# Transposing queries and attention outputs by DMA instead of by matrix engine in a fused attention and expert kernel

## The chip, the cores and the metric

The kernel runs on one core of a Trainium2 chip. The core has five engines with instruction streams of their own: TensorE (PE, matmuls and the weight loads that go before them), VectorE (DVE), ScalarE (ACT), GpSimd (POOL) and SyncE (SP), and 16 DMA engines that move data between HBM and the on-chip memory SBUF. Each instruction stream is worked off strictly in its order. DMAs are started by instructions on a stream: here the plain ones by SP ("SPq" in the profile, hardware queue q1), and those that convert f32 to f16 on the way by POOL (software queue q0). PE writes only to PSUM; what is in PSUM has to be copied ("evacuated") by DVE or ACT before PE or a DMA can use it.

The metric is the time of one execution on the device in microseconds. The median over repeated executions is compared.

## What is computed

The reference is a sorted block attention followed by a mixture of four experts. Cut to what matters:

```python
# q, k, v: (4, 8, 768, 64)   sort_net: (4, 8, 8, 8)
P = sinkhorn(sort_net)                       # 5 rounds of row and column normalisation
k_sorted = einsum('bhij,bhjcd->bhicd', P, k_blocks)     # 8 blocks of 96 tokens
v_sorted = einsum('bhij,bhjcd->bhicd', P, v_blocks)
scores = q_blocks @ k_sorted.T / 8           # inside a block: 96 x 96
attn = softmax(scores)
attn_out = attn @ v_sorted                   # (4, 8, 768, 64)
x = attn_out.transpose(0, 2, 1, 3).reshape(3072, 512)
p = domain_probs / domain_probs.sum(-1)      # (3072, 4)
out = sum(p[:, e] * (relu(x @ w1[e]) @ w2[e]) for e in range(4))   # w1: 512x1024, w2: 1024x512
```

Every token may stand anywhere on the chip, as long as its row of `out` is written to the right place; softmax and the sum over values don't depend on the order of the keys, if values have the same order.

## The kernel before

**Stages.** Four batches. Batch 0 is worked in halves by special functions (`h_k`, `h_v`, `h_s`, `h_a`, `h_x`, `q_half`), because nothing can cover it. Then comes the long stretch in which PE does the expert matmuls of one batch, and the attention of the next batch is cut into small pieces that are put between them. In the first such stage the experts of batch 0 run as twelve-or-so microsecond units (`expert`, lines 540 and 554) with the attention of batch 1 between them. Afterwards batch b runs in three chunks of 256 tokens (`chunk`, lines 620 to 680): eight groups of 16 matmuls of 128x256 into `ps_h` (line 629), each followed by a DVE instruction (line 635) and DVE sums (lines 610 to 616), and then seven products of 16 matmuls into `ps_p` (line 656), combined by DVE, ACT and POOL (lines 669 to 680). The attention of batch b+1 lies between these. The last batch has nothing between.

**Order.** The order of every engine's instructions is the order of the program text (`manual_schedule`); there is no scheduler. `run` hands out "slots": after each group of matmuls `slot()` is called and pops the next pieces of the list `fill`, so many that the list is used up a few slots before the end. `attention_order(b)` makes that list: 24 pieces, v, v, q, k, v, v, and then for each pair of heads `pr` scores (`st_s`), the next pair's `st_q` and `st_k`, attention times values (`st_a`) and the transposition of the result (`st_x`), which is put behind the scores of the next pair.

**The pieces.**
- `st_v` (line 283): two matmuls, evacuated into `vo`; after every second pair SP writes `vo` to a scratch tensor in HBM (`vs_dram`, line 300) and reads it back in another layout (`vs`, line 305). The read waits on SP until the write is complete.
- `st_q` (line 311): 12 PE transposes (matmuls against an identity, line 315) of the queries of a pair of heads into `ps_q`, evacuated into `qT` (line 319), by DVE for batch 1 and by ACT for batches 2 and 3 (`evac`).
- `st_k` (line 322): 12 matmuls that mix and transpose the keys, evacuated into `kT` (line 334).
- `st_s` (line 339): 16 matmuls of `kT` and `qT` (line 344), then exp on ACT (line 351).
- `st_a` (line 368): 16 matmuls (line 376), then per head a reciprocal and a multiplication on DVE, which write `xsl` (lines 360 and 361).
- `st_x` (line 384): 8 PE transposes of `xsl` (line 390) into `ps_x`, evacuated into `xT` (line 393), by the same engine as in `st_q`. `xT` of a batch is what its experts read, in every chunk.

PSUM tiles of these pieces rotate through two buffers (`psA`), those of the experts through two others (`psM`).

**Tokens.** Partition p holds the six consecutive tokens 6p to 6p+5 (`load_natural`, line 79), so rows of 1,536 bytes are read from HBM, 512 of them for a load of four heads. The evacuations undo that order where the blocks of 96 are needed; within `xT` tokens are in the order (r, i, c), and rows of `out` are written with a stride of six rows (line 667).

**Loads.** POOL issues, in this order, the loads of batch 0, w1 and w2 of experts 0 and 1, after the start the k, v and q of batch 1 (lines 723 to 725) and w1 and w2 of experts 2 and 3. Those of batch b+1 are issued by `stage` right after the pieces of batch b that used the buffers (line 502); there are two buffers each. POOL also makes the permutation matrices (`builds`, 4 instructions for a batch) and the sums of w2 blocks for the products (`weight_sums(e)`, 4 instructions each, tile `T_e`).

**Expert weights per token.** `domain_probs` is loaded at the start by SP (lines 168 and 175), normalised by `mix_weights` (5 small DVE instructions) after the first half of batch 0; `spread_weights`, put into the fill list of batch 1 after its tenth piece, transposes it, writes it to `p_dram`, and `load_p` (line 597) reads 512 KB of it for each chunk, broadcast over partitions, into `pb` (one buffer).

Of the kernel before, what the change touches and what calls it, by code (L numbers as in the profile page):

```python
# [17 lines left out]
def kernel(  # L18
# [57 lines left out]

    natural = {}

    def load_natural(b, nm, qd, p0=0, pn=P):
        src = {"q": q, "k": k, "v": v}[nm]  # L80
        if (b, nm, qd) not in natural:
            natural[(b, nm, qd)] = nat.tile([P, 4, R, D], F16, name=f"nat_{nm}_{b}_{qd}", tag=f"nat_{nm}")
        t = natural[(b, nm, qd)]
        nc.gpsimd.dma_start(  # L84
            t[ds(p0, pn)].rearrange("p h r d -> p h (r d)"),
            src[b, ds(4 * qd, 4)].rearrange("h (p r) d -> p h (r d)", r=R)[ds(p0, pn)],
        )

    def head(b, nm, h):
        return natural[(b, nm, h // 4)][:, h % 4, :, :]  # L90
# [33 lines left out]
        eye16.rearrange("p (o c) -> p o c", o=1).broadcast_to([P, NB, CP]),  # L124
    )

    KH = NFC // 2
    Hb = const.tile([P, E, NFC, 2 * P], F16, name="Hb")
    Sb = const.tile([P, 4, E, KH * P], F16, name="Sb")
    Hflat = Hb.rearrange("p e f x -> p (e f x)")  # L130
# [22 lines left out]
    load_w2(0)  # L153
    load_w1(1)
    load_w2(1)
    identf = const.tile([P, P], F32, name="identf")
    nc.gpsimd.tensor_copy(identf[:], ident[:])
    nc.gpsimd.tensor_copy(
        maskv.rearrange("p (c i) -> p c i", i=NB),
        eye16.rearrange("p (c o) -> p c o", o=1).broadcast_to([P, CP, NB]),  # L160
# [1 line left out]
    for n in range(1):  # L162
# [1 line left out]
        nc.gpsimd.memset(vo[:, :, :, ds(D, 2)], 1.0)  # L164
        vos.append(vo)

    p_sb = const.tile([P, B, R, E], F32, name="p_sb")
    nc.sync.dma_start(
        p_sb[:, 1:B].rearrange("p b r e -> p b (r e)"),
        moe_domain_probs.rearrange("(b p r) e -> p b (r e)", b=B, p=P)[:, 1:B],  # L170
    )

    for r2 in range(2):
        for hf in range(2):
            nc.sync.dma_start(
                p_sb[ds(64 * r2, 64), 0, ds(3 * hf, 3), :],
                moe_domain_probs[ds(hf * HS, HS)].rearrange("(p r s) e -> p r s e", r=3, s=2)[:, :, r2, :],
            )

# [100 lines left out]
    def evac(b):  # L280
        return nc.vector.tensor_copy if b == 1 else nc.scalar.copy
# [27 lines left out]
            vss[(b, qd)] = vs  # L309

    def st_q(b, pr):
        ps = psa([P, R, P], F16, f"ps_q_{b}_{pr}")
        for r in range(R):
            for hh in range(2):
                nc.tensor.transpose(  # L315
                    ps[ds(D * hh, D), r, :], head(b, "q", 2 * pr + hh)[:, r, :], ident[:]
                )
        qT = att.tile([P, NB, R, CP], F16, name=f"qT_{b}_{pr}", tag="qT")
        evac(b)(qT[:], ps.rearrange("p r (i c) -> p i r c", c=CP))
        qTs[(b, pr)] = qT.rearrange("p i r c -> p i (r c)")  # L320

    def st_k(b, pr):
        ps = psa([P, R, P], F32, f"ps_k_{b}_{pr}")
# [59 lines left out]

    def st_x(b, pr):
        if b not in xTs:
            xTs[b] = moe.tile([P, NKC, R, NB, CP], F16, name=f"xT_{b}", tag="xT")
        ps = psa([P, NB, BLK], F16, f"ps_x_{b}_{pr}")
        xsl = xsls[(b, pr)]
        for i in range(NB):
            nc.tensor.transpose(  # L390
                ps[:, i, :], xsl[:, i, :, :].rearrange("c h d -> c (h d)"), ident[0:BLK, 0:BLK]
            )
        evac(b)(
            xTs[b][:, pr, :, :, :].rearrange("p r i c -> p i r c"),
            ps.rearrange("p i (r c) -> p i r c", c=CP),
        )


# [86 lines left out]
    def attention_order(b):  # L485
        o = [(st_v, 0), (st_v, 1), (st_q, 0), (st_k, 0), (st_v, 2), (st_v, 3)]
        for pr in range(NPB):
            o.append((st_s, pr))
            if pr + 1 < NPB:
                o += [(st_q, pr + 1), (st_k, pr + 1)]  # L490
            o.append((st_a, pr))
            o.append((st_x, pr))

        for pr in range(NPB - 1):
            o.remove((st_x, pr))
            o.insert(o.index((st_s, pr + 1)) + 1, (st_x, pr))

        def stage(f, pr):
            f(b, pr)
            nm = {st_q: "q", st_k: "k", st_v: "v"}.get(f)  # L500
            if nm and pr % 2 and b + 1 < B:
                load_natural(b + 1, nm, pr // 2)

        return [lambda f=f, pr=pr: stage(f, pr) for f, pr in o]

    NR = (B - 1) * E * R
    p_dram = dramp.tile([B - 1, E, R * P], F32, name="p_dram")
    pn = const.tile([P, NR], F32, name="pn")  # L510
    pT = const.tile([NR, P], F32, name="pT")

    def spread_weights():
        ps = psa([NR, P], F32, "ps_p")
        nc.tensor.transpose(ps[:], pn[:], identf[:])
        nc.vector.tensor_copy(pT[:], ps[:])
        nc.sync.dma_start(p_dram.rearrange("b e (r p) -> (b e r) p", p=P), pT[:])
        pbs[(1, 0)] = load_p(1, 0)

    def mix_weights():  # L520
        den = const.tile([P, B, R, 1], F32, name="den")
        nc.vector.tensor_reduce(den[:], p_sb[:], AX.X, ALU.add)
        nc.vector.tensor_scalar(out=den[:], in0=den[:], scalar1=1e-9, scalar2=None, op0=ALU.add)
        nc.vector.reciprocal(den[:], den[:])
        nc.vector.tensor_tensor(p_sb[:], p_sb[:], den[:].broadcast_to([P, B, R, E]), ALU.mult)
        nc.vector.tensor_copy(pn.rearrange("p (b e r) -> p b r e", b=B - 1, e=E), p_sb[:, 1:B])

    oaccs = {}

    def expert(b, e, hf, slot):  # L530
# [19 lines left out]
        for t in range(n // P):  # L550
            col = (R // 2) * hf + t
            ps = psm([P, Dm], F32, f"ps_o_{b}_{e}_{col}")
            for fc in range(NFC):
# [1 line left out]
                    ps[:], hT[:, fc, ds(t * P, P)], w2sb[e][:, fc, :],  # L555
                    start=(fc == 0), stop=(fc == NFC - 1),
                )
            pcol = p_sb[:, b, col, ds(e, 1)]
            if e == 0:
                oaccs[(b, col)] = moeo.tile([P, Dm], F32, name=f"oacc_{b}_{col}", tag="oacc")  # L560
                nc.vector.tensor_scalar(
# [14 lines left out]

    DH = Dm // 2
    Ts = []  # L580

    def weight_sums(e):
        t = const.tile([P, 3, KH, DH], F16, name=f"T_{e}")
        w = w2sb[e]
        b11, b12 = w[:, 0:KH, 0:DH], w[:, 0:KH, DH:Dm]
        b21, b22 = w[:, KH:NFC, 0:DH], w[:, KH:NFC, DH:Dm]
        t2, t3, n4 = t[:, 0], t[:, 1], t[:, 2]
        tt = nc.gpsimd.tensor_tensor
        tt(t3, b22, b12, ALU.subtract)
        tt(b12, b12, b11, ALU.subtract)  # L590
        tt(t2, b22, b12, ALU.subtract)
        tt(n4, b21, t2, ALU.subtract)
        Ts.append({
            "b11": b11, "b21": b21, "b22": b22, "t1": b12, "t2": t2, "t3": t3, "n4": n4,
        })

    def load_p(b, c):
        pb = moe.tile([P, E, 2 * P], F32, name=f"pb_{b}_{c}", tag="pb", bufs=1)
        nc.sync.dma_start(
            pb[:],  # L600
            p_dram[b - 1, :, ds(2 * c * P, 2 * P)].rearrange("(o e) x -> o e x", o=1).broadcast_to([P, E, 2 * P]),
        )
        return pb

# [14 lines left out]

    def chunk(b, c, slot):  # L620

        xT = xTs[b].rearrange("p k r i c -> p k (r i c)")
        pb = pbs.pop((b, c))
        for e in range(E):
            for g in range(2):
# [38 lines left out]
        ob = moeo.tile([P, Dm], F32, name=f"ob_{b}_{c}", tag="oacc")  # L664
        p1, p5, u2, u3 = [moe.tile([P, DH], F32, name=f"{n}_{b}_{c}", tag=n, bufs=1) for n in ("p1", "p5", "u2", "u3")]
        tt = nc.vector.tensor_tensor
        o = out[ds(b * S, S), :].rearrange("(p r) d -> p r d", r=R)
        oa1, oa2, ob1, ob2 = oa[:, 0:DH], oa[:, DH:Dm], ob[:, 0:DH], ob[:, DH:Dm]
        nc.scalar.copy(p1[:], product("p1", blk(0, 0), "b11"))  # L669
        nc.scalar.copy(ob1, product("p4", blk(1, 1), "n4"))  # L670
# [42 lines left out]
    h_x(0, 0, nc.scalar.copy)  # L713
    h_a(1, 0)
    h_x(1, 0, nc.scalar.copy)
    mix_weights()
    state["start"] = False

    build_PI0(nc.gpsimd, 1, Rs[:, 0:H, HB:NB])
# [1 line left out]
        build_PI(nc.gpsimd, n, "v")  # L721
        build_PI(nc.gpsimd, n, "k")
    for qd in range(2):
        for nm in ("k", "v", "q"):
            load_natural(1, nm, qd)
    for e in range(2, E):
        load_w1(e)
        load_w2(e)
# [64 lines left out]
```

## Time and profile before

| what | value |
|---|---|
| median of 5 runs | 404.31 us (402.59 to 404.64) |
| the profiled execution, its own time | 404.2 us |
| its span on the core | 402.4 us |
| mean granted TensorE clock | 0.975 |
| instructions | 8931 |
| DMA packets, bytes | 34,059 packets, 34.38 MB |
| q0 (POOL's queue): packets, share of the 16 engines' span | 18,976, 29.2% |
| q1 (SP's queue): packets, share | 15,044, 13.3% |

The profile counts microseconds from the start of the span. The stages in it: batch 0's attention up to about 62.7, with its first expert units from 29.2 on; expert units of batch 0 with the attention of batch 1 from 62.7 to 137.2; the chunks of batch 1 with the attention of batch 2 from 137.2 to 228.0; the chunks of batch 2 with the attention of batch 3 to 318.6; the chunks of batch 3 alone to 398.5; the last outputs up to the end.

The groups that the change touches, each with its count, busy time and mean duration:

| line | engine, what | count | busy us | mean ns |
|---|---|---|---|---|
| 315 | PE transposes into `ps_q` | 144 | 6.3 | 223 |
| 390 | PE transposes into `ps_x` | 96 | 6.1 | 206 |
| 319 | ACT copies `qT` (batches 2, 3) | 8 | 6.4 | 799 |
| 319 | DVE copies `qT` (batch 1) | 4 | 2.2 | 552 |
| 393 | ACT copies `xT` (batches 2, 3) | 8 | 6.4 | 799 |
| 393 | DVE copies `xT` (batch 1) | 4 | 2.2 | 550 |
| 84 | POOL, issuing loads of q | 10 | 7.0 | 713 |

A matmul's mean duration is the time from its start to its modelled end; matmuls overlap, so 12 of them take far less than 12 times that, and what a group costs PE is read from the starts of the groups before and after it.

### The profile page before, as it was taken

How to read it: one execution, taken by the hardware profiler on the slowest of the kernel's cores; microseconds unless marked ns; L12 is line 12 of the kernel's file. 1: busy time of each engine (PE TensorE's matmuls, PEld its weight loads, DVE VectorE, ACT ScalarE, POOL GpSimd, SP SyncE). 2: the span in 40 equal slices, each digit the busy share in tenths (PEclk: the TensorE clock that was granted, in tenths of full speed). 3: DMA queues.
4: the chain of work that ended last, by engine and by line, in shares of the span. 5: the costliest groups of instructions: out<-in, count | busy, mean ns of one | idle time of the engine just before them, and what ended most of it. 6: DMA issues, size and time to landing. Idle time of an engine off the chain costs nothing.

```text
span 402.4 us, 8931 instructions
## 1 busy us (share of the span) xinstructions
PE 383.8 (95%) x3965; PEld 301.0 (75%) x3965; DVE 233.5 (58%) x418; ACT 93.8 (23%) x140; POOL 89.8 (22%) x107
## 2 busy tenths in 40 slices
PE   4779989999999999999999999999999999999996
PEld 4665555555555688888888888888888888888885
DVE  5462443452444385397388386397388395693772
ACT  2253243223432223132312123232312001000000
POOL 8452030049459430200200500100100100101001
PEclk9658999999999999999999999999999999999999
DMA  9999999993063364911151123201101101101101
GB/s 120 207 210 194 129 148 203 199 205 83 0 79 81 78 121 108 154 46 52 56 78 54 54 82 92 94 2 54 55 2 53 53 2 54 54 0 54 55 0 54
DMA packets 34059, 34.38 MB, mean 85 GB/s; under 512 B 2652, under 2 KB 28324, under 8 KB 34020
## 3 DMA queue, kind: packets, MB, share of 16 engines
q0 software_dynamic: 18976, 17.83, 29.2%
q1 hardware_dynamic: 15044, 15.97, 13.3%
q8 instruction: 31, 0.51, 0.5%
q14 instruction: 8, 0.07, 0.0%
HBM read 42.86 MB, written 8.76 MB: 128 GB/s over the span
## 4 chain that ended last, share of the span: by engine, by line
PE 82%; DVE 10%; DMA 4%; ACT 1%; issue 1%; POOL 0%; DVEq 0%; SPq 0%; ACTq 0%; POOLq 0%
PE ps_h L629 27%; PE ps_p L656 26%; PE ps_o L554 9%; PE ps_h L540 9%; DVE Hb L635 3%; DMA vs_dram<-vo 3%; DVE xsl L361 2%; DMA nat_q<-in_q_dram 2%; PE ps_k L327 1%; PE ps_q L315 1%; PE ps_s L344 1%; PE ps_w L187 1%; PE ps_x L390 1%; PE ps_a L376 1%; PE ps_v L287 1%
## 5 line engine op out<-in xcount | busy, mean ns | idle before, releaser
L629 PE MATMUL ps_h<-xT,w 128*128 128x256 f16 x1152 | 132.0, 273 | 1.0 <-DVE Hb L635 1.0
L629 PEld LDWEIGHTS <-w 128*128 128x128 f16 x1152 | 111.2, 98 | 16.0 <-issue 1.2
L635 DVE SCALAR_TENSOR_TENSOR Hb<-ps_h,pb 128x1024 f16<-128x1024 f32 x72 | 87.7, 1220 | 24.4 <-PE ps_h L629 24.3
L656 PEld LDWEIGHTS <-Sb 128*128 128x128 f16 x576 | 55.6, 98 | 7.0
L674 POOL TENSOR_TENSOR oa<-u,p 128x256 f32<-128x256 f32 x9 | 6.5, 724 | 202.9 <-issue 177.9
L540 PE MATMUL ps_h<-xT,w 128*128 128x384 f16 x256 | 47.3, 333 | 0.2 <-ACT xT L480 0.2
L656 PEld LDWEIGHTS <-Hb 128*128 128x128 f16 x432 | 41.7, 98 | 5.9 <-issue 0.6
L554 PE MATMUL ps_o<-w,Hb 128*128 128x512 f16 x192 | 44.4, 380 | 0.0
L546 ACT ACTIVATE Hb<-ps_h 128x768 f16<-128x768 f32 x32 | 26.0, 811 | 62.7 <-PE ps_h L540 62.7
L540 PEld LDWEIGHTS <-w 128*128 128x128 f16 x256 | 24.1, 99 | 16.2 <-issue 1.6
L656 PE MATMUL ps_p<-w,Sb 128*128 128x256 f16 x288 | 34.4, 273 | 0.0
L656 PE MATMUL ps_p<-w,Hb 128*128 128x256 f16 x288 | 34.4, 273 | 0.0
L656 PE MATMUL ps_p<-T,Sb 128*128 128x256 f16 x288 | 33.3, 273 | 0.0
L554 PEld LDWEIGHTS <-Hb 128*128 128x128 f16 x192 | 17.6, 98 | 19.8 <-ACT Hb L546 0.6
L565 DVE SCALAR_TENSOR_TENSOR oacc<-ps_o,p_sb,oacc 128x512 f32<-128x512 f32 x18 | 13.5, 750 | 26.8 <-PE ps_o L554 26.8
L351 ACT ACTIVATE ET<-ps_s 96x768 f16<-96x768 f32 x24 | 18.0, 802 | 36.3 <-PE ps_s L344 36.3
L361 DVE TENSOR_TENSOR xsl<-ps_a,rz 96x512 f16<-96x512 f32 x32 | 22.0, 687 | 1.1
L673 DVE TENSOR_TENSOR u<-ps_p,p 128x256 f32<-128x256 f32 x9 | 3.8, 425 | 30.4 <-PE ps_p L656 30.4
L669 ACT COPY p<-ps_p 128x256 f32<-128x256 f32 x9 | 3.4, 374 | 74.3 <-PE ps_p L656 64.3
L656 PE MATMUL ps_p<-T,Hb 128*128 128x256 f16 x144 | 17.2, 272 | 0.1
L612 DVE TENSOR_TENSOR Sb<-Sb,Hb 128x512 f16<-128x512 f16 x36 | 15.3, 425 | 1.2
L84 POOL DMA_DIRECT2D nat_v<-in_v_dram x8 | 6.1, 758 | 41.0 <-PE ps_v L287 34.5
(104 smaller groups left out, 353.9 us busy)
## 6 DMA issues: line engine op xcount, KB each, us to landing
w<-in_moe_w_dram POOLq DMA_DIRECT2D x8, 1024.0 KB, 17.7
pb<-p_dram SPq DMA_DIRECT2D x9, 512.0 KB, 4.0
nat_k<-in_k_dram POOLq DMA_DIRECT2D x8, 384.0 KB, 6.5
nat_v<-in_v_dram POOLq DMA_DIRECT2D x8, 384.0 KB, 7.4
vs_dram<-vo SPq DMA_DIRECT2D x6, 396.0 KB, 4.2
vs<-vs_dram SPq DMA_DIRECT2D x6, 396.0 KB, 4.6
nat_q<-in_q_dram POOLq DMA_DIRECT2D x6, 384.0 KB, 5.9
out_dram<-ob SPq DMA_DIRECT2D x9, 256.0 KB, 2.1
```

What stands on the lines that cost most here:

```text
L84: nc.gpsimd.dma_start(t[ds(p0, pn)].rearrange("p h r d -> p h (r d)"), src[b, ds(4 * qd, 4)].rearrange("h (p r) d -> p h (r d)", r=R)[ds(p ...
L351: nc.scalar.activation(ETs[2 * (pr % 2) + hh][:, 0:S].rearrange("c (a x) -> c a x", a=2), pss[hh][0:BLK, :, 0:HS], AF.Exp, bias=0.0, scale ...
L361: nc.vector.tensor_tensor(xsl[:, :, hh, :].rearrange("c (a i) d -> c a i d", a=2), av[:, :, :, 0:D], rz[:].broadcast_to([BLK, 2, HB, D]), ...
L540: nc.tensor.matmul(ps[:, a, 0:HS], w1sb[e][:, kc, ds((2 * f2 + a) * P, P)], xT0[hf][:, :, kc, :], start=(kc == 0), stop=(kc == NKC - 1),)
L546: nc.scalar.activation(hT[:, ds(2 * f2, 2), :], ps[:, :, 0:HS], AF.Relu, bias=0.0, scale=1.0,)
L554: nc.tensor.matmul(ps[:], hT[:, fc, ds(t * P, P)], w2sb[e][:, fc, :], start=(fc == 0), stop=(fc == NFC - 1),)
L565: nc.vector.scalar_tensor_tensor(out=oaccs[(b, col)][:], in0=ps[:], scalar=pcol, op0=ALU.mult, in1=oaccs[(b, col)][:], op1=ALU.add,)
L612: tt(sm[1], sm[0], blk(0, 0), ALU.subtract)
L629: nc.tensor.matmul(ps[:, f, :], w1sb[e][:, kc, ds((4 * g + f) * P, P)], xT[:, kc, ds(2 * c * P, 2 * P)], start=(kc == 0), stop=(kc == NKC ...
L635: nc.vector.scalar_tensor_tensor(out=Hb[:, e, ds(4 * g, 4), :], in0=ps[:], scalar=0.0, op0=ALU.max, in1=pb[:, ds(e, 1), :].broadcast_to([P ...
L656: nc.tensor.matmul(ps[:], lhs(e, f), Ts[e][rhs][:, f, :], start=(e == 0 and f == 0), stop=(e == E - 1 and f == KH - 1),)
L674: nc.gpsimd.tensor_tensor(oa2, u2[:], p5[:], ALU.add)
```

## The change

- `st_q` no longer uses PE, PSUM, DVE or ACT. SP issues one transposing DMA from the loaded queries (128 x 768 f16) into `qT` (128 x 6 x 128). `qT` has three buffers instead of two.
- `st_x` likewise: one transposing DMA from `xsl` (96 x 1024) into its quarter of `xT` (128 x 8 x 96).
- Queries of batches 1 to 3 are loaded by `load_queries`: partition p holds tokens p, 128+p, ..., so that the transposed queries come out in natural order. That takes one DMA for each head (8 a batch instead of 2) with rows of 256 bytes in HBM and 128 bytes in SBUF, into one buffer. Those of batch 1 come after k and v of batch 1 and before the weights of experts 2 and 3; those of batch b+1 are issued after the last `st_s` of batch b.
- `xT` and `out` of batches 1 to 3 are in natural token order: a store of 128 tokens writes 128 consecutive rows.
- The expert weights per token of batches 1 to 3 are loaded in natural order by one SP DMA of 2,304 rows of 16 bytes (before: 384 rows of 96 bytes) and normalised in `spread_weights`; those of batch 0 are normalised where all were before.
- To make room, the queries of batch 0 lie in tile `T_3`, and the f32 identity and the weights per token in tile `T_2`, until `weight_sums` writes these.

In the program, the two transposing DMAs stand in SP's stream where `st_q` and `st_x` stand in the order of pieces. SP's stream in the attention of batch 1 begins: write of `vs_dram`, read of `vs`, transposition of pair 0's queries, write, read, transposition of pair 1's queries, write of `p_dram`, load of `pb`, transposition of pair 0's outputs, and so on.

```diff
+    def load_queries(b):
+        t = nat.tile([P, NPB, R, 2, D], F16, name=f"natq_{b}", tag="natq", bufs=1)
+        natural[(b, "q")] = t
+        for h in range(H):
+            nc.gpsimd.dma_start(t[:, h // 2, :, h % 2, :], q[b, h].rearrange("(t p) d -> p t d", p=P))
...
     def st_q(b, pr):
-        ps = psa([P, R, P], F16, f"ps_q_{b}_{pr}")
-        for r in range(R):
-            for hh in range(2):
-                nc.tensor.transpose(
-                    ps[ds(D * hh, D), r, :], head(b, "q", 2 * pr + hh)[:, r, :], ident[:]
-                )
-        qT = att.tile([P, NB, R, CP], F16, name=f"qT_{b}_{pr}", tag="qT")
-        evac(b)(qT[:], ps.rearrange("p r (i c) -> p i r c", c=CP))
-        qTs[(b, pr)] = qT.rearrange("p i r c -> p i (r c)")
+        qT = att.tile([P, R, P], F16, name=f"qT_{b}_{pr}", tag="qT", bufs=3)
+        nc.sync.dma_start_transpose(
+            qT[:], natural[(b, "q")][:, pr].rearrange("p t h d -> p (t h d)")
+        )
+        qTs[(b, pr)] = qT.rearrange("p t x -> p (t x)").rearrange("p (i x) -> p i x", i=NB)
...
     def st_x(b, pr):
         if b not in xTs:
-            xTs[b] = moe.tile([P, NKC, R, NB, CP], F16, name=f"xT_{b}", tag="xT")
-        ps = psa([P, NB, BLK], F16, f"ps_x_{b}_{pr}")
-        xsl = xsls[(b, pr)]
-        for i in range(NB):
-            nc.tensor.transpose(
-                ps[:, i, :], xsl[:, i, :, :].rearrange("c h d -> c (h d)"), ident[0:BLK, 0:BLK]
-            )
-        evac(b)(
-            xTs[b][:, pr, :, :, :].rearrange("p r i c -> p i r c"),
-            ps.rearrange("p i (r c) -> p i r c", c=CP),
+            xTs[b] = moe.tile([P, NKC, NB, BLK], F16, name=f"xT_{b}", tag="xT")
+        nc.sync.dma_start_transpose(
+            xTs[b][:, pr], xsls[(b, pr)].rearrange("c i h d -> c (i h d)")
         )
...
+            if f == st_s and pr == NPB - 1 and b + 1 < B:
+                load_queries(b + 1)
...
+    def load_weights_of_tokens():
+        nc.sync.dma_start(pn, moe_domain_probs[S:N].rearrange("(t p) e -> p t e", p=P))
+
     def spread_weights():
+        normalized(pn, NT, "den_1")
...
-        o = out[ds(b * S, S), :].rearrange("(p r) d -> p r d", r=R)
+        o = out[ds(b * S, S), :].rearrange("(t p) d -> p t d", p=P)
...
     for qd in range(2):
-        for nm in ("k", "v", "q"):
+        for nm in ("k", "v"):
             load_natural(1, nm, qd)
+    load_queries(1)
```

## The prediction

> **What bounds the kernel now.** I read the page's engine shares and the shares of the chain of waits, then the windows by stage.
>
> ```profile
> PE 383.8 (95%) x3965; PEld 301.0 (75%) x3965; DVE 233.5 (58%) x418; ACT 93.8 (23%) x140; POOL 89.8 (22%) x107
> ...
> PE 82%; DVE 10%; DMA 4%; ACT 1%; issue 1%; POOL 0%; DVEq 0%; SPq 0%; ACTq 0%; POOLq 0%
> ```
>
> ```profile
> 62.70:137.20 74.50, 74.17 (x602) 40.50 (x601) 31.76 (x51) 24.96 (x32) 36.57 (x24) 1.00 0.62 113
> 137.20:227.95 90.75, 90.19 (x986) 77.96 (x985) 59.76 (x103) 21.87 (x33) 15.01 (x16) 1.00 0.39 80
> ```
>
> The second view gives, for a stretch, its length, then busy microseconds of PE, PEld, DVE, ACT and POOL, the granted clock, the share of the DMA engines and GB/s. In both stages that hold the pieces to be replaced PE is idle for 0.3 and 0.6 us. A piece taken from PE there shortens the time by its own length, unless PE then waits.
>
> **What the pieces cost PE.** Timeline of the second chunk of batch 1 (start, length, instructions), PE lines:
>
> ```profile
> 192.04 1.91 PE L656 MATMUL ps_p<-T,Sb 128*128 128x256 f16 x16
> 193.79 0.51 PE L390 MATMUL ps_x<-ident,xsl 96*128 96x96 f16 x8
> 194.13 1.91 PE L656 MATMUL ps_p<-T,Sb 128*128 128x256 f16 x16
> 195.88 1.91 PE L656 MATMUL ps_p<-w,Sb 128*128 128x256 f16 x16
> 197.72 0.53 PE L315 MATMUL ps_q<-ident,nat_q 128*64 128x128 f16 x12
> 198.18 1.92 PE L629 MATMUL ps_h<-xT,w 128*128 128x256 f16 x16
> ```
>
> Sixteen matmuls take 1.75 from start to start (194.13 to 195.88). With `st_x` between it is 2.09 (192.04 to 194.13), with `st_q` 2.30 (195.88 to 198.18): the pieces cost 0.34 and 0.55. There are 12 of each: 12 x 0.89 = 10.7 us off PE.
>
> Not all of it is gained. In the chain in order of time the steps from 204.2 to 218.8, and again from 294.9 to 309.5, are DVE's (lines 635 and 361), which the change doesn't relieve there. One `st_x` lies in each: 2 x 0.34 = 0.7 stays.
>
> The evacuations, 8 x 0.55 on DVE for batch 1 and 16 x 0.80 on ACT, are priced at nothing: DVE has 31.8 us of work in the 74.5 us of the first stage, ACT 21.9 in 90.8, and PE waited for neither. Fewer `psA` tiles only loosen their rotation.
>
> **What comes in their place.** A transposing DMA occurs nowhere in this trace. Its row of bounds: the shortest SP transfer lands in 2.1 us (256 KB stores), the longest in 10.7 (the first `vs_dram` write, 768 rows under load). Nearest by rows and size is that write without load, 3.4 us (issued 233.11, its reader released at 236.47); I take 3.0 for what one adds when it stands in a queue already running.
>
> Most have cover. `st_x` of the last pair is the tight one:
>
> ```profile
> 218.12 0.69 DVE L361 TENSOR_TENSOR xsl<-ps_a,rz 96x512 f16<-96x512 f32 x1
> 218.86 0.37 PEld L390 LDWEIGHTS <-xsl 96*128 96x128 f16 x8 [0.35 <-DVE xsl L361]
> 227.95 1.25 PE L629 MATMUL ps_h<-xT,w 128*128 128x256 f16 x10
> ```
>
> `xsl` is ready at 218.8 and the next chunk reads `xT` at 227.95: 9.1 us, hidden by five products; 9.1 in the next stage, 8.6 before the first chunk (128.65 to 137.23). Queries of batches 2 and 3 have 14 us from `st_q` (145.0) to `st_s` (159.0). SP issues the `vs` read at 146.0; it lands 4.8 later and the transposition by 154. So 0.
>
> The first pair of batch 1 is not covered:
>
> ```profile
> 67.21 0.40 SPq L300 DMA_DIRECT2D vs_dram<-vo  x1
> 68.66 0.53 PE L315 MATMUL ps_q<-ident,nat_q 128*64 128x128 f16 x12
> 77.90 0.33 SPq L305 DMA_DIRECT2D vs<-vs_dram  x1
> 79.51 0.21 PE L344 MATMUL ps_s<-qT,kT 64*128 64x96 f16 x1
> 79.86 0.36 SPq L300 DMA_DIRECT2D vs_dram<-vo  x1
> ```
>
> ```profile
> vs_dram<-vo SPq DMA_DIRECT2D x1, 396.0 KB, 10.7
> ...
> vs<-vs_dram SPq DMA_DIRECT2D x1, 396.0 KB, 7.7
> ...
> vs_dram<-vo SPq DMA_DIRECT2D x1, 396.0 KB, 7.0
> ```
>
> (The last view: DMA issues of the three SP lines above, KB, and us to landing.) PE made these queries at 68.7, ten microseconds ahead. In the new stream the transposition stands behind the `vs` read, which SP holds until the write has landed, so it is issued at 78.2. The read lands at 85.6. The write issued after it, at 79.86, landed at 86.9, only 1.3 behind: what follows in SP's queue comes in after what stands before. So the queries land at 85.6 + 3.0 = 88.6. PE reaches the scores at 79.5 - 0.55 + 0.4 (start, below) = 79.4 and stands for 9.2 us, and behind it in PE's order all expert matmuls. Bounds: 0.9, if the transposition passes the read and takes 2.1; 16.9, if it takes 10.7 behind it. The next pair gains from that stall: its transposition is out at about 93 and lands by 98, PE is there at 92.5 - 1.1 + 9.6 = 101: 0.
>
> A standing PE loses clock. Windows of the start, when PE became continuously busy at 30.3:
>
> ```profile
> 30.00:32.00 2.00, 1.75 (x7) 0.71 (x5) 0.00 (x0) 0.25 (x1) 0.00 (x0) 0.50 1.16 207
> 32.00:34.00 2.00, 2.00 (x40) 1.34 (x39) 0.70 (x2) 0.81 (x1) 0.08 (x1) 0.54 1.27 215
> 34.00:36.00 2.00, 2.00 (x35) 1.24 (x33) 0.62 (x1) 0.81 (x2) 0.79 (x2) 1.00 1.19 195
> ```
>
> The clock stays at 0.50 for 3.7 us of full work, which loses 1.9. I add 1.9 (bounds 0 and 1.9).
>
> [...]
>
> **Loads and the rest.** Queries: 6,144 rows a batch instead of 1,024. Between 113 and 125 us 1,056 q0 packets took 51.1% of 16 engines: 93 ns each at 1,536 bytes; between 2 and 12 us 1,235 small q1 packets took 11.5%: 15 ns each. A batch thus occupies every engine for 5.8 to 36 us (before 6.0); nearest are the 528-byte rows at 50 ns (896 packets, 25.3% of 11 us), scaled down to 30: 11.5, 5.5 more. Behind them on POOL stand w1 of expert 2, landed at 61.9 and first used at 88.4: 26 us of cover, lost by some 5 us only at the upper bound. POOL's six more issues of 0.75 are 4.5 us. Behind those of batch 2 stand `weight_sums(2)` and `builds`, whose first result (125.0 to 126.0) is used at 139.0: covered. Those of batch 3 come well before `oa` (line 674 at 225). They wait for all four transpositions of the batch before, which PE needs earlier anyway.
>
> The 2,304 rows of 16 bytes are issued at the start, when the first queries set the chain (landing at 8.5). Turn by turn with the 48 packets an engine of the first k and q loads (512 + 256 rows over 16) they add 48 x 15 ns = 0.7, and the 384 rows that go give back 0.36: +0.4 (bounds -0.3 and +1.5). Normalising later moves five DVE instructions of 1.2 us together to about 91 us; behind them `pb`, issued at 93.6 and first read at 139.2: 0. Behind the transpositions on SP stand also `pb` loads (issued 216.5, read 229.9) and stores: covered. `T_2` and `T_3` are free at about 91 and 50, written from 116 on: 0. Rows of `out` keep their 2 KB: 0.
>
> **Sum**, against the profiled run's own 404.2 (span 402.4 and 1.8 around it; 0.1 under the median): 404.2 - 10.7 + 0.7 + 0.4 = 394.6 with no stall; + 9.2 + 1.9 = **405.7**.
>
> **The rivals.**
> - *The stall is short* (faster). The queries pass the `vs` read, land like an unloaded write at 78.2 + 3.4 = 81.6, and PE stands 2.2 us without losing clock: 394.6 + 2.2 = 396.8. For it: the read's rows are few and long, and transposing traffic may not share its turns. Against: the 1.3 us between read and next write. It decides if they land before 86.5 (stall 7.1, with the clock 403.6).
> - *Transposing is slow* (slower). At 10.7 each, PE stands 16.9 + 1.9, and `xT` is late before three batches: 10.7 - 8.6 + 0.3, and twice 10.7 - 9.1 + 0.3: 6.2 in all; 419.6. It decides from about 8.6 on. For it: nothing in the trace shows its speed; against: twice the bytes take 3.4 as a copy.
> - *The removed work was not PE's to give*: DVE sets the pace throughout the chunks and 394.6 becomes 401.7 (2 x 3.56 lost), 412.8 with stall. Against: DVE works 59.8 of 90.75 us there.
>
> **How the numbers follow.** Forecast (stall between 7 and 13 us) 0.50, short stall 0.30, slow transposing 0.17, pace of DVE 0.03. The forecast's own range is 403 to 411. What this kernel's measurement can tell is about 0.3%, 1.2 us. Of the forecast's 0.50 I put 0.03 below 403.1, 0.17 within and 0.30 above 405.5; with the rivals faster 0.33, same 0.17, slower 0.50. The range goes from 396.5, which takes in most of the short stall, to 417, short of the slowest.
>
> **What would show it.** Lines 315 and 390 gone from PE and some 3.6 us less PE time in each stage; PE's `ps_s` of batch 1's first pair held by the DMA of `qT` for about 9 us near 79, with a clock of 0.50 after it; transpositions landing about 3 us after what stands before them; no wait of line 629 for `xT`. A `qT` wait under 3 us, or `xT` waits at the starts of batches, would make the prediction wrong.

## The result, and the profile after

| kernel | median | range | runs |
|---|---|---|---|
| before | 404.1 us | 402.27 to 406.13 | 50 |
| after | 406.62 us | 403.36 to 408.16 | 26 |

The ratio of after to before is 1.0054, with a 95% interval of 1.0039 to 1.0068: slower by half a per cent. Below, "before" and "after" stand for the two kernels. The profiled execution of after has a span of 404.8 us; the one of before has 402.4.

Engine shares and the shares of the chain of waits, page of after:

```profile
PE 377.1 (93%) x3725; PEld 294.9 (73%) x3725; DVE 231.8 (57%) x413; ACT 81.6 (20%) x124; POOL 105.1 (26%) x125
...
PE 84%; DVE 7%; DMA 6%; ACT 1%; issue 1%; POOL 0%; SPq 0%; DVEq 0%; ACTq 0%; POOLq 0%
```

PE works 6.7 us less than before (383.8), on 240 matmuls fewer, ACT 12.2 us less; and the span is longer. The work that went was not idle work, so PE must have waited somewhere instead. The windows by stage of after (stretch, its length, busy us of PE, PEld, DVE, ACT and POOL, granted clock, DMA share, GB/s) say in which stage:

```profile
61.77:146.60 84.83, 74.89 (x523) 39.38 (x522) 31.05 (x47) 25.07 (x32) 39.99 (x29) 0.92 0.75 119
146.60:234.05 87.45, 86.74 (x906) 75.51 (x905) 59.81 (x103) 15.67 (x25) 21.86 (x23) 1.00 0.60 101
234.05:321.15 87.10, 86.60 (x906) 75.53 (x905) 59.74 (x103) 15.67 (x25) 8.23 (x10) 1.00 0.28 74
```

The two stages of chunks are shorter by 3.30 (90.75 before) and 3.55 us (90.65). The first stage is longer by 10.33 (74.50): PE stands there for about 10 us, and the clock falls to 0.92 in the mean. With the start (0.93 us earlier in this execution) and the last stage (83.65 instead of 83.80) this adds up to the whole difference of the spans: -0.93 + 10.33 - 3.30 - 3.55 - 0.15 = 2.4.

The timeline of PE in after, where before went on at 79.5 with the scores:

```profile
75.31 2.76 PE L548 MATMUL ps_h<-xT,w 128*128 128x384 f16 x16
84.94 0.82 PE L351 MATMUL ps_s<-qT,kT 64*128 64x96 f16 x16 [6.87 <-DMA qT<-natq]
85.69 2.74 PE L548 MATMUL ps_h<-xT,w 128*128 128x384 f16 x8
88.23 4.92 PE L562 MATMUL ps_o<-w,Hb 128*128 128x512 f16 x16
...
101.42 0.40 PE L530 MATMUL ps_p<-T 128*72 128x128 f32 x1 [2.90 <-DVE T L515]
101.62 2.76 PE L548 MATMUL ps_h<-xT,w 128*128 128x384 f16 x8
```

Two waits, in brackets with what ended them. The first is the one that was looked for, 6.87 us for the transposed queries. The second, 2.90 us for the normalised weights per token, is a surprise. Behind each the same matmuls take longer than before: 16 scores 0.82, 8 of `ps_h` 2.74 and 16 of `ps_o` 4.92 us, against 0.51, 1.47 and 3.63, which is 2.9 us; behind the second wait 2.76 for 8 against 1.46 and 0.40 for one against 0.27, 1.4 us. PE in before, at the same places (its first score ran alone, at 79.51):

```profile
79.88 0.50 PE L344 MATMUL ps_s<-qT,kT 64*128 64x96 f16 x15 [0.16 <-DVE vo L294]
80.31 1.47 PE L540 MATMUL ps_h<-xT,w 128*128 128x384 f16 x8
...
82.17 3.63 PE L554 MATMUL ps_o<-w,Hb 128*128 128x512 f16 x16
...
91.12 1.46 PE L540 MATMUL ps_h<-xT,w 128*128 128x384 f16 x8
```

The windows of after show why, by the granted clock (the figure after POOL's): it fell during the wait and came back about 6 us after it.

```profile
80.00:82.00 2.00, 0.00 (x0) 0.00 (x0) 0.00 (x0) 0.00 (x0) 0.00 (x0) 0.65 1.20 298
82.00:84.00 2.00, 0.00 (x0) 0.00 (x0) 0.00 (x0) 0.00 (x0) 0.00 (x0) 0.50 1.30 130
84.00:86.00 2.00, 1.06 (x18) 0.75 (x19) 0.00 (x0) 0.21 (x1) 0.00 (x0) 0.50 0.88 204
...
90.00:92.00 2.00, 2.00 (x9) 0.86 (x8) 0.54 (x1) 0.00 (x0) 0.00 (x0) 0.79 0.34 62
```

So the first stage saves its 4 x 0.89 = 3.6 us and loses 6.87 + 2.9 + 2.90 + 1.4 = 14.1: 10.5, and 10.33 are seen.

SP's queue in after, and what its transfers of 64 to 79 us took from issue to landing (the last figure):

```profile
66.27 0.37 SPq L311 DMA_DIRECT2D vs_dram<-vo  x1
77.21 0.33 SPq L316 DMA_DIRECT2D vs<-vs_dram  x1
77.65 1.33 SPq L324 DMA_TRANSPOSE qT<-natq  x1
```

```profile
vs_dram<-vo SPq DMA_DIRECT2D x1, 396.0 KB, 10.9
vs<-vs_dram SPq DMA_DIRECT2D x1, 396.0 KB, 7.0
qT<-natq SPq DMA_TRANSPOSE x1, 7.2
```

The value write holds the read until 77.2, the transposition goes out right behind the read and lands at 77.65 + 7.2 = 84.9, only 0.7 us after the read (77.21 + 7.0 = 84.2).

The second wait, in the timelines of DVE and of POOL in after (lines 512 to 515 normalise the weights per token, lines 597 and 598 belong to `weight_sums`):

```profile
97.81 0.21 DVE L512 TENSOR_REDUCE den<-T 128x18 f32<-128x72 f32 x1
98.06 0.97 DVE L513 TENSOR_SCALAR den<-den 128x18 f32<-128x18 f32 x1
99.06 0.27 DVE L514 RECIPROCAL den<-den 128x18 f32<-128x18 f32 x1
99.36 1.91 DVE L515 TENSOR_TENSOR T<-T,den 128x72 f32<-128x72 f32 x1
```

```profile
96.87 2.12 POOL L597 TENSOR_TENSOR w<-w 128x1024 f16<-128x1024 f16 x1
99.07 2.11 POOL L598 TENSOR_TENSOR T<-w 128x1024 f16<-128x1024 f16 x1
```

DVE's line 513 ends at 99.03 and POOL's 597 at 98.99; DVE's 515 ends at 101.27 and POOL's 598 at 101.18. Two DVE instructions end with the POOL instruction that runs beside them. Lines 512 and 514 between them take 0.21 and 0.27.

### The profile page after: what moved, and what is told of

Read it like the earlier page. It is cut to its first block, busy times and chain, and to the rows that moved or that the text cites. A ratio compares the mean times of both kernels' runs of the same rounds, so it can differ in the third digit from the quotient of the medians.

```text
span 404.8 us, 8510 instructions
## 1 busy us (share of the span) xinstructions
PE 377.1 (93%) x3725; PEld 294.9 (73%) x3725; DVE 231.8 (57%) x413; ACT 81.6 (20%) x124; POOL 105.1 (26%) x125
## 3 DMA queue, kind: packets, MB, share of 16 engines
q1 hardware_dynamic: 36161, 20.70, 21.1%
## 4 chain that ended last, share of the span: by engine, by line
PE 84%; DVE 7%; DMA 6%; ACT 1%; issue 1%; POOL 0%; SPq 0%; DVEq 0%; ACTq 0%; POOLq 0%
PE ps_h L636 29%; PE ps_p L663 28%; PE ps_o L562 9%; PE ps_h L548 9%; DMA vs_dram<-vo 3%; DVE xsl L368 2%; DMA qT<-natq 2%; DVE Hb L642 2%; DMA T<-in_q_dram 1%; PE ps_k L334 1%; PE ps_s L351 1%; PE ps_w L198 1%; PE ps_a L383 1%; PE ps_v L298 1%; DVE kT L417 1%
## 5 line engine op out<-in xcount | busy, mean ns | idle before, releaser
L636 PEld LDWEIGHTS <-w 128*128 128x128 f16 x1152 | 111.9, 98 | 16.5 <-issue 2.1
L548 PE MATMUL ps_h<-xT,w 128*128 128x384 f16 x256 | 49.7, 345 | 0.2 <-ACT xT L480 0.2
L663 PEld LDWEIGHTS <-Hb 128*128 128x128 f16 x432 | 41.8, 98 | 5.9 <-issue 0.6
L548 PEld LDWEIGHTS <-w 128*128 128x128 f16 x256 | 25.0, 102 | 17.7 <-issue 3.5
L562 PEld LDWEIGHTS <-Hb 128*128 128x128 f16 x192 | 18.4, 100 | 21.8 <-issue 2.0
L103 POOL DMA_DIRECT2D natq<-in_q_dram x24 | 19.7, 860 | 0.4 <-issue 0.4
L93 POOL DMA_DIRECT2D nat_k<-in_k_dram x8 | 6.4, 794 | 45.5 <-PE ps_k L334 35.0
```

What stands on the lines that cost most here:

```text
L93: nc.gpsimd.dma_start(t[ds(p0, pn)].rearrange("p h r d -> p h (r d)"), src[b, ds(4 * qd, 4)].rearrange("h (p r) d -> p h (r d)", r=R)[ds(p ...
L103: nc.gpsimd.dma_start(t[:, h // 2, :, h % 2, :], q[b, h].rearrange("(t p) d -> p t d", p=P))
L548: nc.tensor.matmul(ps[:, a, 0:HS], w1sb[e][:, kc, ds((2 * f2 + a) * P, P)], xT0[hf][:, :, kc, :], start=(kc == 0), stop=(kc == NKC - 1),)
L562: nc.tensor.matmul(ps[:], hT[:, fc, ds(t * P, P)], w2sb[e][:, fc, :], start=(fc == 0), stop=(fc == NFC - 1),)
L636: nc.tensor.matmul(ps[:, f, :], w1sb[e][:, kc, ds((4 * g + f) * P, P)], xT[:, kc, ds(2 * c * P, 2 * P)], start=(kc == 0), stop=(kc == NKC ...
L663: nc.tensor.matmul(ps[:], lhs(e, f), Ts[e][rhs][:, f, :], start=(e == 0 and f == 0), stop=(e == E - 1 and f == KH - 1),)
```

## The experiments

The kernel before, on the same chip and at the same time, took 403.33 us for the first four runs, 403.87 for the next four and 403.83 for the last four; every ratio is against that. As the runs before differ by up to 0.2% from the 404.1 above, a difference to the changed kernel is taken from the ratios: 1.0054 less the run's own, times 404.1; each has an uncertainty of about 1 us.

### The first two transpositions ahead of the stage

```diff
     first = attention_order(1)
+    for n in (2, 7):              # st_q of pairs 0 and 1
+        first[n]()
+        first[n] = lambda: None
```

> The transpositions of pairs 0 and 1 of batch 1's queries stand ahead of all vs_dram transfers on SP, all else as in the changed kernel. Theory (the stall came from standing behind the vs write and read on SP): they land before 70 us, PE's wait of 6.9 us for qT and the half clock after it (2.9 us) go, 406.6 - 9.8 = 396.8. Rival (the load on the DMA engines by weights near 78 us, or another transfer the scores need, holds PE just as long): PE still stands near 78 us, time within 2 us of 406.6.

Measured: 399.59 us, ratio 0.9907 (0.9887 to 0.9928), 5.9 us under the changed kernel. The wait for `qT` is gone. Another, smaller one stands in the same place (PE timeline):

```profile
80.78 0.20 PE L351 MATMUL ps_s<-qT,kT 64*128 64x96 f16 x1 [1.38 <-DVE vo L305]
81.64 0.50 PE L351 MATMUL ps_s<-qT,kT 64*128 64x96 f16 x15 [0.67 <-DVE vo L305]
82.07 2.49 PE L548 MATMUL ps_h<-xT,w 128*128 128x384 f16 x8
```

The scores take over the PSUM buffers that DVE's `vo` copies empty, and these wait for the value write, which landed 12.1 us after its issue at 67.56. Before had that wait too, with 0.16 us. These waits and the slow matmuls behind them (2.49 and 4.33 us against 1.47 and 3.63) make 3.8 us, which is what is missing from the 9.8 expected. The queries were not the only thing that is late here: what delays the write is the next limit.

The second wait stays, at 2.90 us, but in this execution the matmuls behind it have their full speed (1.46 us for the 8 of `ps_h`, 0.27 for the one of `ps_p`): the same wait cost clock in after and none here.

### The normalisation early

```diff
     load_weights_of_tokens()
+    normalized(pn, NT, "den_1")
...
     def spread_weights():
-        normalized(pn, NT, "den_1")
```

> The weights per token of batches 1 to 3 are normalised directly after those of batch 0 (near 29 us) instead of in spread_weights; the query stall stays. Theory (PE's wait of 2.9 us for the normalised weights and the half clock after it cost some 4.2 us, because two of the DVE instructions wait for POOL's sums): DVE lines 513 and 515 take 0.2 to 0.3 us each, no wait of the transposition of the weights above 0.3 us, 406.6 - 4.2 = 402.4. Rival (the wait is part of the recovery from the query stall and PE only waits elsewhere): within 1 us of 406.6.

Measured: 401.3 us, ratio 0.9951 (0.9935 to 0.9967). In the new place, near 28.5 us, POOL is idle, and the two instructions take 0.18 and 0.23 us. PE goes from the matmuls before `ps_p` straight on, and the wait for `qT` stays, at 7.58 us. By the ratios this gives back 4.2 us; the trace of after had 2.90 + 1.4 = 4.3.

### Both together

> Both edits. Theory (the two waits are separate and add): 406.6 - 9.8 - 4.2 = 392.6, under the kernel before by 11.5 us; PE idle under 1 us in the stage from 62 us to the first chunk. Rival (with PE earlier the next thing is late: outputs of batch 1 not transposed in time, or POOL's permutation matrices): one of these waits appears before the first chunk, time above 395.

Measured: 396.6 us, ratio 0.9823 (0.9795 to 0.9852), 4.0 over the 392.6 expected. The two gains add up, nearly: 5.9 and 4.2 alone, 9.3 together. What is left of the stalls is PE's 1.16 and 0.66 us for `vo`, which neither expectation named, with a clock down to 0.50 from 82 to 84 us.

### The transposition ahead of the value read

```diff
     def st_v(b, pr):
...
             nc.sync.dma_start(vs_dram...)          # the write
+            if (b, pr) == (1, 1):
+                st_q(1, 0)
...
             nc.sync.dma_start(vs...)               # the read
...
     first = attention_order(1)
+    first[2] = lambda: None
```

> Only pair 0's transposition is moved, to between the vs write and the vs read on SP, so that it is issued near 67 us while the write is under way for 11 us. Theory (SP's transfers land in the order of the queue): it lands with the write or under 1.5 us after it, near 77 to 79 us, and not in the 3 to 4 us of an unloaded transposition; PE's wait at the scores is under 1 us; 396.5 to 398.5. Rival (each transfer has its own share of the engines and only their load counts): it lands well before the write, at 70 to 74 us.

Measured: 403.27 us, ratio 0.9987 (0.9961 to 1.0013), and a wait of 4.30 us. Neither expectation holds: the queries land 4.8 us after the write (66.99 + 11.3 = 78.3), not with it and not well before it. SP's line, the landing, and the packets of the two queues between 79 and 81 us:

```profile
67.46 5.08 SPq L326 DMA_TRANSPOSE qT<-natq  x1
```

```profile
qT<-natq SPq DMA_TRANSPOSE x1, 15.6
```

```profile
q0 software_dynamic: 332, 0.26, 89.2%
q1 hardware_dynamic: 332, 0.08, 42.7%
```

Issued ten microseconds sooner, the queries come only 1.8 sooner: 67.46 + 15.6 = 83.1. SP is held for 5.08 us by the issue alone.

Two things hold the transposition. One is its place behind the write: from 72 to 77 us q1 moved 691 packets beside 692 of q0, but only 102 of all these were under 512 bytes. The transposition's packets have 256 bytes and the write's 528 (by their sizes in the trace of after), so nearly all were the write's. Small packets came in number only when the write was almost through: 173 from 77 to 79 us, 348 from 79 to 81, 228 from 81 to 83. The other is the load: beside the backlog in POOL's queue q0, SP's packets of q1 went one for one with it (the 691 beside 692, and 332 beside 332 in the view above), and the change makes some 800 packets for a transposition ((36,161 - 15,044 - 1,920 more rows of weights per token) / 24). Here they take from 76 to 83 us; in after nearly all of them went between 82 and 84 us, when q1 moved 763 packets beside 75 of q0.

### PE kept at work while it waits

```diff
+    scores = first[6]
+    first[6] = lambda: (warm(112), scores())
```

> 112 matmuls that nothing reads are put on TensorE just ahead of the scores of pair 0, batch 1, so that it works through most of the 6.87 us in which it waits for qT; nothing else is changed. Theory (the wait costs twice: its own length and the half clock behind it): qT still lands at about 85 us, the scores still start within 1 us of that, but the 8 and 16 matmuls behind them (2.74 and 4.92 us in the changed kernel) take 1.5 and 3.7 us again, so about 2.9 us come back: 406.6 - 2.9 = 403.7 us. Rival (the slow matmuls have another cause, such as DMA traffic or the evacuations): they stay slow and the time stays at 406.6 us.

Measured: 403.05 us, ratio 0.9986 (0.9962 to 1.0009): 2.7 us under the changed kernel, 2.9 expected. PE timeline:

```profile
78.20 6.41 PE L198 MATMUL ps_w<-ident 128*128 128x128 f16 x112 [0.31 <-DVE vo L305]
84.97 0.51 PE L351 MATMUL ps_s<-qT,kT 64*128 64x96 f16 x16 [0.36 <-DMA qT<-natq]
85.42 1.47 PE L548 MATMUL ps_h<-xT,w 128*128 128x384 f16 x8
86.73 3.62 PE L562 MATMUL ps_o<-w,Hb 128*128 128x512 f16 x16
```

The scores start at 84.97 as they did at 84.94, so nothing came sooner; what runs behind them has the lengths of before again. The slow matmuls were the price of standing still, not of DMA traffic. The second wait is still 2.90 us here, and as in the first run the matmuls behind it are not slow (1.46 us for 8).

### The sums of weights written later

Shortened:

```diff
-        + plain(weight_sums 0, 1) + halves([(0, 2, 0), (0, 2, 1), (0, 3, 0)])
+        + halves([(0, 2, 0)]) + plain(weight_sums 0, 1) + halves([(0, 2, 1), (0, 3, 0)])
```

> The eight GpSimd instructions that make the sums of the weights of experts 0 and 1 are put behind one more half-unit of the feed-forward; the normalisation stays where the change has it. Theory (VectorE's instructions on fp32 tiles wait until GpSimd's tensor instruction ends): L513 and L515 take 0.2 to 0.3 us in their place instead of 0.97 and 1.91, TensorE's wait for the normalised weights falls from 2.90 to about 0.6 us and the half clock behind it (about 1.3 us) goes, so 406.6 - 3.6 = 403.0 us, less what the sums may cost where they now stand. Rival (the normalisation is slow where it stands whatever GpSimd does, or the place in the order alone costs the wait): L513 and L515 stay near 1 and 1.9 us and the time stays at 406.6 us.

Measured: 406.16 us, ratio 1.0061 (1.0033 to 1.0089), and this tells nothing about the cause. POOL began the sums at 94.05 us as before (94.66): it had nothing else to do, so a later place in the program did not make them later. Lines 513 and 515 took 0.96 and 1.92. A later run, below, does what this one meant to.

### The weights of expert 3 later

Shortened:

```diff
-    for e in range(2, E):
-        load_w1(e); load_w2(e)
+    load_w1(2); load_w2(2)
...
         halves([(0, 0, 1), (0, 1, 1)])
+        + plain(lambda: load_w1(3), lambda: load_w2(3))
```

> The 2 MB of weights of expert 3 are asked for about 38 us later (behind the half-unit of expert 1, at about 92 us, for a use at about 120 us); nothing else is changed. Theory (the small rows of the value write, of its read and of the transposition take turns packet by packet with GpSimd's loaded queue, and that is why they take 11, 7 and 7 us): the queue is empty some 10 us sooner, the value write issued at about 67 us lands in 4 to 7 us instead of 11, the transposition is issued at 72 to 75 us and lands 3 to 5 us later, before or within 1 us of 79.4 us, when TensorE comes to the scores; the 6.87 us and the half clock behind them go: 397 to 399 us. Rival (the transposition is late because SP hands it out behind the value write and read and because it is slow by itself): write and transposition keep their 11 and 7 us, the wait stays over 5 us and the time at 405 to 407 us. If the weights of expert 3 land too late for their use, TensorE waits there and the time says so.

Measured: 396.66 us, ratio 0.9837 (0.9814 to 0.986), 8.8 us under the changed kernel where 6.87 + 2.9 = 9.8 was to be had (397 to 399 us expected). SP's queue, the landings of its transfers issued from 72 to 77 us, the landing of the write, and PE:

```profile
66.79 0.38 SPq L311 DMA_DIRECT2D vs_dram<-vo  x1
71.71 0.33 SPq L316 DMA_DIRECT2D vs<-vs_dram  x1
72.15 1.82 SPq L324 DMA_TRANSPOSE qT<-natq  x1
```

```profile
vs<-vs_dram SPq DMA_DIRECT2D x1, 396.0 KB, 4.0
...
qT<-natq SPq DMA_TRANSPOSE x1, 4.4
```

```profile
vs_dram<-vo SPq DMA_DIRECT2D x1, 396.0 KB, 4.9
```

```profile
78.53 0.51 PE L351 MATMUL ps_s<-qT,kT 64*128 64x96 f16 x16
78.98 1.47 PE L548 MATMUL ps_h<-xT,w 128*128 128x384 f16 x8
```

Write, read and transposition take 4.9, 4.0 and 4.4 us instead of 10.9, 7.0 and 7.2, in the same order of the queue and with the same work. The queries are there at 76.6, PE comes at 78.5 and doesn't wait. So the place behind write and read is dear only with the backlog: 2 MB of weights, which after first uses at 123 us, stood in POOL's queue beside them. POOL now issues them at 85 to 87 us, and PE doesn't wait for them. Either cure ends the wait for `qT`: the transposition out of that place (the first run) or the backlog out of the way (this one). The change didn't make the backlog: in before the value write took 10.7 us at the same place. It put a transfer that PE waits for behind it.

The wait for the normalised weights stays (2.34 us), without slow matmuls behind it.

### All three

> The first two transpositions of queries ahead of the stage, the normalisation early, and the weights of expert 3 later, together. Theory: what the run with the first two left (TensorE waits 1.16 and 0.66 us for vo at 79 to 80 us, and a clock of 0.5 to 0.7 behind it) came from the value write beside the loaded queue, and goes: 396.6 - 2.8 = 393.8 us. Rival: the wait for vo is set by something else, and the time stays at 396.6 us.

Measured: 393.49 us (393.19 to 394.7), ratio 0.9756 (0.9734 to 0.9777). This version beats both kernels. Its windows by stage:

```profile
62.10:133.53 71.43, 71.26 (x526) 38.23 (x525) 27.80 (x44) 24.85 (x32) 41.59 (x31) 1.00 0.90 142
133.53:220.98 87.45, 86.73 (x905) 75.49 (x904) 59.82 (x103) 15.67 (x25) 21.85 (x23) 1.00 0.58 101
220.98:308.10 87.12, 86.62 (x907) 75.54 (x905) 59.79 (x104) 15.67 (x25) 8.30 (x10) 1.00 0.27 74
```

Now the first stage is 3.07 us shorter than before (74.50) at a clock of 1.00, and the chunk stages are as in after (87.45 and 87.10 there). The waits for `vo` are gone too, so they came from the same backlog: the value write lands after 4.6 us, against 12.1 in the first run.

### The sums held behind the normalisation

```diff
         normalized(pn, NT, "den_1")
+        after_it = const.tile([P, 1, E], F32, name="after_it")
+        nc.gpsimd.tensor_copy(after_it[:], pn[:, 0:1, :])
```

on top of the kernel with the sums written later.

> In the run before it the GpSimd sums of the weights of experts 0 and 1 were only written one half-unit later; GpSimd was free and began them at 94 us all the same. Here one small GpSimd copy that reads the normalised weights stands ahead of them, so that they can't begin before the normalisation has ended. Theory (VectorE's fp32 instructions wait for GpSimd's running tensor instruction): L513 and L515 take 0.2 to 0.3 us, TensorE's wait for the normalised weights falls from 2.90 to 0.3 to 0.8 us and the half clock behind it goes: 406.6 - 2.3 - 1.3 = 403.0 us (within 1 us). Rival (they are slow in this place of VectorE's order whatever GpSimd does): 0.97 and 1.9 us stay, and 406.6 us.

Measured: 402.41 us, ratio 0.996 (0.9943 to 0.9976), 3.8 us under the changed kernel, 3.6 expected. DVE and PE:

```profile
98.64 0.18 DVE L513 TENSOR_SCALAR den<-den 128x18 f32<-128x18 f32 x1
...
99.15 0.23 DVE L515 TENSOR_TENSOR T<-T,den 128x72 f32<-128x72 f32 x1
```

```profile
99.53 0.27 PE L532 MATMUL ps_p<-T 128*72 128x128 f32 x1 [0.43 <-DVE T L515]
99.64 1.46 PE L550 MATMUL ps_h<-xT,w 128*128 128x384 f16 x8
```

In the same place of DVE's order, with POOL waiting (its copy runs at 99.45, its sums from 99.60) instead of working, the two take 0.18 and 0.23 us, and PE's wait is 0.43. It was POOL's work, not the place.

### Before, with the weights of expert 3 later

The edit of "The weights of expert 3 later", in the kernel before.

> The kernel before, with the weights of expert 3 asked for later in the same way. Theory (it has no transposition by DMA, and TensorE stood little in its first stage): 403.9 us stays, within 1 us, and the gain of this cure belongs to the changed kernel alone; the change is then worth about 10 us once its stalls are gone. Rival (the emptier queue helps the first stage of any of these kernels): 400 us or less.

Measured: 403.18 us, ratio 0.9975 (0.9959 to 0.9992). By the ratio the kernel before gains 1.0 us (0.3 to 1.7), by the medians 0.6 (403.83 - 403.18); little in it waited for SP's queue. So with its stalls gone the change is worth 403.18 - 393.49 = 9.7 us by the medians, (0.9975 - 0.9756) x 404.1 = 8.8 by the ratios.

### Either half of the change alone

Both start from the version of 393.49 us. One transposes the queries by PE again (and so has no early transpositions), one the outputs, each with its evacuations. The edit for the queries, shortened (that for the outputs is of the same kind, with 8 transposes):

```diff
     def st_q(b, pr):
-        nc.sync.dma_start_transpose(qT[:], ...)
+        ps = psa([P, R, P], F16, f"ps_q_{b}_{pr}")
+        ... 12 nc.tensor.transpose ...
+        evac(b)(qT[:], ps[:])
```

> The kernel of the three cures (393.5 us), with the queries of batches 1 to 3 transposed by TensorE and evacuated as before the change, from the same natural tiles; the outputs stay with the DMA. Theory (a piece is worth its TensorE time, 12 pieces of 0.55 us, and the evacuations are hidden): 393.5 + 6.6 = 400.1 us, within 1 us. Rival (part of it is hidden, or its evacuations cost too): under 398 or over 402 us.

> The kernel of the three cures (393.5 us), with the attention outputs of batches 1 to 3 transposed by TensorE and evacuated as before the change; the queries stay with the DMA. Theory: 12 pieces of 0.34 us, less 0.7 us for two pieces in stretches that VectorE paces: 393.5 + 3.4 = 396.9 us, within 1 us. Rival (the piece waits for its evacuations too, or TensorE is not the pace there): under 395.5 or over 399 us.

Measured: 399.4 us (399.05 to 399.64), ratio 0.9876 (0.9851 to 0.9901), with queries on PE: over the 393.49 it costs 5.9 us by the medians and 4.8 by the ratios, for 12 pieces. 396.07 us (395.95 to 397.16), ratio 0.9801 (0.9774 to 0.9828), with outputs on PE: 2.6 by the medians and 1.8 by the ratios. Together 8.5 or 6.7, beside 9.7 or 8.8 for all; where the 1.2 to 2.1 us between them lie, no run shows. Both medians are within 1 us of what was expected, on its lower side: nothing shows that an evacuation cost anything, and some of the PE time may have been hidden.

## Why the prediction was right in its time, and where it was wrong

The forecast was 405.7 us and slower; 406.62 was measured. The likeliest case came in, with its place and cause: PE stands at the scores of batch 1's first pair, and the queries land behind the `vs` read. But several terms were off, and they nearly cancel: that the sum came within 1 us is in part luck.

- **What the change takes off PE: right.** -10.7 + 0.7 was forecast. The chunk stages gave 3.30 + 3.55 = 6.85 against 7.12 - 0.7 = 6.4 for both, and the change without stalls is worth 8.8 to 9.7, beside 10.0. The evacuations at nothing held, and so did the time that was to hide `st_x` and the queries of batches 2 and 3: line 636 never waits for `xT`, and no queries are waited for after the first pair.
- **The stall: mechanism right, size too large.** 9.2 forecast, 6.87 measured. The read landed 6.1 us after PE's arrival (78.07 to 84.2), 6.2 in the forecast; what was mis-sized is the 3.0 for the transposition behind it, which took 0.7. (Its row of bounds is off too: the shortest SP transfer of before took 1.6 us, the 8 KB of `sn`, not 2.1; the sum doesn't use it.) What made the read late, and with it the queries, was the backlog of weights, which the forecast took over with the read's landing. By the forecast's own limit this is hardly its case: it was to hold for a stall of 7 to 13, and the short stall took over below 7.1 or with a landing before 86.5, and the queries landed at 84.9. Without the cost of the normalising, below, the time would have been 402.3, under that border.
- **Half clock: 1.9 forecast, 2.9 measured** by the matmuls behind the wait; removing it alone brought 2.7. The 3.7 us of the start (nearer 3.5 by its rows, with 0.54 from 32 to 34) were too short a model: here the clock was low until about 91, 6 us after the first matmul. The size differs from one execution to the next: in three other runs with this wait the same matmuls lost 2.3 (normalisation early), 2.6 (sums later) and 2.8 us (sums held).
- **"Normalising later moves five DVE instructions of 1.2 us together ...; behind them `pb` ...: 0": this step failed.** It looked at who reads `pb`, and not at PE, whose transposition of these weights stands at this point of its stream, and not at what POOL does there. The four of them that stand there (lines 512 to 515) took 3.5 us (97.81 to 101.27), PE stood 2.90, and the clock brought it to 4.3 in the profiled execution; moving them away gave back 4.2, holding POOL back 3.8.
- **Start: +0.4 forecast, -0.93 in the profile.** That isn't a gain of the change: the first expert matmul of before came at 29.21 us in one execution, and at 28.41 in the run with only expert 3's weights later, whose start is the same code. In after and the runs made from it, it came between 28.32 and 29.22. The start differs by that much from one execution to the next, and the 0.4 can't be told in it.

Summed up: -2.3 (stall) + 1.0 (clock) + 4.3 (normalising) - 1.3 (start) - 0.6 (chunks and last stage 7.0 instead of 6.4) = +1.1, which with 405.7 is 406.8.

The price of a transposition, which no row of before showed: in after the twelve of queries had a median of 3.7 us from issue to landing and those of outputs 3.0, and behind a running read one added 0.7. The 192 KB of one took about as long as the 396 KB of a `vs` write or read (medians 4.3 and 3.7 in after), and longer than a plain store of 256 KB (2.0 to 2.3).

**The rivals.** Slow transposing (419.6) fell: the longest landing in after was 7.2, under load, and at the same place in the emptier queue 4.4. (The 15.6 of the run between write and read began behind the write.) DVE as the pace fell: both chunk stages became shorter by PE's share. The short stall (2.2 us, 396.8) was further off than the forecast: 6.87 lies just inside its border of 7.1, but the queries didn't pass the `vs` read. No case had the normalising wait.

## What to carry to other kernels

Moving work from an engine to a DMA makes the result's time a question of what else is in the DMA queues at that minute (here 7.2 us to the landing with a backlog beside it, 4.4 without): look for bulk loads that are asked for long before their use, and move these before you move the small transfer. When a change moves small instructions, ask who stands behind them in the order of every engine that reads their result, and which POOL instruction runs beside them (here 0.97 and 1.91 us beside a sum of weights, 0.18 and 0.23 without). Where TensorE is made to wait, count the slow matmuls that may come behind the wait as well (here 2.9 us behind one of 6.87).

## What the runs showed of the hardware

- **DVE beside POOL.** In after a DVE fp32 `TENSOR_SCALAR` of 128x18 and a `TENSOR_TENSOR` of 128x72 took 0.97 and 1.91 us with a POOL tensor instruction running; in the run with the sums held behind the normalisation, POOL waiting, they took 0.18 and 0.23. A `TENSOR_REDUCE` and a `RECIPROCAL` between them weren't held: 0.21 and 0.27 in both runs. Why these two and not the others isn't shown.
- **SP's issue of a transposition** takes 1.2 us in the median of after (1.21 to 1.85), against 0.32 to 0.43 for a `vs` or `pb` transfer, and 5.08 in the one run where it stood right behind the value write, with SP's stream held. Load alone doesn't make it long: the issue at 77.65 in after took 1.33. What does isn't shown.
- **The clock falls after short stands too, but not each time.** In the run with both edits together, with waits of 1.16 and 0.66 us, 0.2 apart, it was 0.69 and 0.50 in the next 4 us. With expert 3's weights later it stayed at 1.00 after a wait of 2.34 us, and after the same 2.90 us the matmuls were slow in after (2.76 us for 8) and not in the first run and the run that kept PE at work (1.46). The length of the wait alone doesn't sort these; what decides it stays open.
- **How the two queues share.** In three stretches beside a backlog they went one for one: 656 of q1 beside 656 of q0 from 70 to 75 us in after, and 691 beside 692 from 72 to 77 and 332 beside 332 from 79 to 81 us in the run with the transposition ahead of the read. From 79 to 81 us in after it was 21 beside 494, but that is no share: the read, issued at 77.21, moved nothing before 80 us (none beside 274 of q0 from 79 to 80). The write of after, issued at 66.27, moved nothing before 69.5 either; with expert 3's weights later it was issued at 66.79, and q1 moved 784 packets from 67 to 72 us, against 261 in after. Why the first packets came so late beside the backlog isn't shown. Without the backlog write, read and transposition took 4.9, 4.0 and 4.4 us instead of 10.9, 7.0 and 7.2.
